# Reordering the opening of a convolution and maxout feed-forward kernel: products, zeroing, casts and two loads

## The chip, the core and the metric

The kernel runs on one core of a Trainium2 chip. TensorE multiplies matrices into PSUM; VectorE, ScalarE and GpSimd do elementwise work on SBUF (VectorE and ScalarE also on PSUM); SyncE issues the transfers between HBM and SBUF. The engines run side by side, each through its own queue in order, and wait for each other on semaphores. The metric is the device time of one execution in microseconds. Before the change the median of three runs is 453.2 us (452.73 to 454.73).

## What is computed

A short causal convolution along the sequence, with a softmax over its seven taps for each of eight heads, feeds a three-way maxout layer and an output projection. Cut to what matters:

```python
# x: (8, 4160, 192), weight: (8, 7), w1, w2, w3: (192, 768), w_out: (768, 192)
w = softmax(weight, axis=-1)
x_pad = concat([zeros(8, 6, 192), x], axis=1)
y[b, s, h*24 + g] = sum(w[h, k] * x_pad[b, s + k, h*24 + g] for k in range(7))
y = y.reshape(33280, 192)
h = maximum(maximum(y @ w1, y @ w2), y @ w3)
out = h @ w_out          # (33280, 192), float32
```

## The kernel before, in words

The 33,280 tokens are cut into 65 blocks of 512. For every block the kernel makes y (the convolution), then six hidden tiles of 128 columns, then four output tiles of 128 tokens.

**The algebra.** max(y w1, y w2, y w3) is y w3 + max(relu(y(w1 - w3)), y(w2 - w3)). So `wd` holds w1 - w3 and w2 - w3 as fp16 (made by `make_wd`, from the float32 weights in `wall`, whose parts are `ws` and `w3s`), and the y w3 w_out part is one 192x192 matrix `m16` made once: w3 is cast (`cast_w3`), transposed on TensorE (`transpose_w3`), multiplied by w_out (`make_m`) and copied out by ScalarE. A hidden tile takes two PSUM banks: ScalarE computes r = relu of one, VectorE takes the maximum with the other into h (`top`). Stage 2 multiplies h by w_out and adds y m16.

**The 192 columns.** The 192 input channels are 128 plus 64. A full product uses 128 rows of the array; the remaining 64 channels of both factors run as two half-height products side by side. `wd` therefore has slots 0 and 1 (first 128 channels of either factor), slot 2 (the last 64 of both, one in each half of the partitions) and slot 3, in which `cross_wd` puts copies of parts of slots 0 and 1 in the other half. For slot 2 w3 must stand in both partition halves: `copy_w3` does that. Blocks 0 and 1 use the full-height "first products" (`l1_dense` part "F") and half-height "third products" (part "H"); from block 2 on, `l1` uses half-height products throughout, and so needs slot 3 and the same kind of copy of y (`cross`).

**The opening.** Blocks 0 to 3 are loaded dense (`load_x`), cast to fp16 with zeros between channels (`cast_dense`, into two buffers `xz`, shared by blocks 0 and 2, and by 1 and 3), convolved by matmuls with a band matrix in two halves (`conv_dense`, tile D; the first half holds channels 0 to 127) and evacuated to `yd`. Blocks 4 onward are loaded into seven rotating buffers `xf`, some rows of which must be zeroed before the load (`zero_x`), then cast by GpSimd (`cast_x`), convolved (`conv`), evacuated and turned by a transposing transfer (`turn`). `first_hidden` is stage 2 of block 0 (24 products of h and w_out), `first_rest` adds the y m16 part later. `keep_warm` issues idle matmuls at the very start.

**What sets the order.** The order is written out by hand for the opening: each engine executes its instructions in program order. In the loop that follows, two lanes of half-height products are interleaved by column count. All loads are on SyncE's queue, in order; an issue waits until the transfer eight issues earlier is complete, and a load of x4 to x7 also waits for its buffer's zeroing. PSUM is three pools: psp and psq with two banks each, psw with four. `PQ` names psp and psq; `WW` names psw twice.

Before the change, the opening runs in this order: first differences of weights, conv 0, zeroing of x6, loads of x4 to x6, cast of block 1 by GpSimd and ScalarE, first products of block 0's hidden tiles 0 and 1, conv 1 (second half first), third products of those tiles, block 1's tiles 0 and 1, then tiles 2 and 3 and tiles 4 and 5 of both blocks, the transposition of w3, stage 2 of block 0, conv 2, m, and the loop.

Of the kernel before, what the change touches and what calls it, by code (L numbers as in the profile page):

```python
# [28 lines left out]
def kernel(  # L29
# [12 lines left out]
    nc = tc.nc  # L42
# [3 lines left out]
    H, KWs = weight.shape  # L46
# [39 lines left out]
    NDENSE = 4  # L86
# [3 lines left out]
    NR = NBLK // TOK // 2  # L90
# [28 lines left out]
    xin, xbuf, XBUF, loaded = {}, [], 7, set()  # L119

    def get_x(t):

        if not 0 <= t < NB or t in xin:
            return
        if t < XBUF:
            xbuf.append(const.tile([P, NR, D], FP32, name=f"xf_{t}"))
        xf = xbuf[t % XBUF if t < NDENSE + XBUF else NDENSE + (t - NDENSE - XBUF) % 3]
        assert all(v[0] is not xf for v in xin.values())
        xin[t] = [xf, 0, ()]

    def zero_x(t, q0=0, q1=NR, eng=None):

        if t >= NDENSE:
            get_x(t)
        xf = xbuf[t]
        if eng is not None:
            eng.memset(xf[TOK:HALF, q0:q1, :], 0.0)
            return
        zero = idle[TOK:HALF, 0:D]
        nc.scalar.copy(out=xf[TOK:HALF, q0:q1, :],  # L140
                       in_=bass.AP(tensor=zero.tensor, offset=zero.offset,
                                   ap=[list(zero.ap[0]), [0, q1 - q0], [1, D]]))

    def load_x(t, eng=nc.sync):
        if not 0 <= t < NB:
            return
        loaded.add(t)
        get_x(t)
        xf = xin[t][0]
        if t < NDENSE:  # L150
            todo = [(0, c[3], c[1] * SEQ + c[2], i) for i, c in enumerate(chunks_of[t])]
        else:
            todo = [(HALF * (i // NR) + (0 if s else LAP), KR if s else TOK,
                     b * SEQ + s - (LAP if s else 0), i % NR) for i, (b, s) in enumerate(rows_of(t))]
        parts = []
        i, n = 0, len(todo)
        row = [c[2] for c in todo]
        while i < n:
            k = i
            while k + 1 < n and todo[k + 1][:2] == todo[i][:2] and row[k + 1] - row[k] == row[i + 1] - row[i]:  # L160
                k += 1
            step = row[i + 1] - row[i] if k > i else 0
            p0, rlen, _, q0 = todo[i]
            q1 = todo[k][3] + 1
            src = bass.AP(tensor=x.tensor, offset=row[i] * D,
                          ap=[[D, rlen], [step * D, q1 - q0], [1, D]])
            eng.dma_start(out=xf[p0:p0 + rlen, q0:q1, :], in_=src)  # L167
            if parts and parts[-1][0] == rlen:
                parts[-1] = (rlen, parts[-1][1], q1)
            else:  # L170
                parts.append((rlen, q0, q1))
            i = k + 1
        xin[t] = [xf, todo[0][0], parts]
# [33 lines left out]
    def cast_dense(t, copies, slots_=range(CYC // 32)):  # L207
        xf, _, parts = xin.pop(t)
        for v, copy in enumerate(copies):
            if copy is None:  # L210
                continue
            for s in slots_:
                cut = GRP * (32 * s // GRP + 1)
                a, b = (32 * s, cut) if v == 0 else (cut, 32 * s + 32)
                for (rl, q0, q1) in parts:
                    copy(  # L216
                        out=xz[t][v][0:rl, q0:q1, :].rearrange("p q (k c) -> p q k c", c=CYC)[:, :, :, a:b],
                        in_=xf[0:rl, q0:q1, :].rearrange("p q (k c) -> p q k c", c=CYC)[:, :, :, a:b])
# [8 lines left out]
    def load_wa(f):  # L227
        for st, n, wsrc in ((w3s, 0, moe_w3), (ws, 0, moe_w1), (ws, 1, moe_w2)):
            nc.sync.dma_start(out=st[:, n, f], in_=wsrc[0:P, f])  # L229
# [15 lines left out]
    load_wa(slice(PW, 2 * PW))  # L245
    load_wb(slice(PW, DFF))
    load_wa(slice(2 * PW, DFF))
    nc.sync.dma_start(out=wos[:], in_=moe_w_out.rearrange("(j p) c -> p j c", p=P))
    load_x(2)
    load_x(3)  # L250
    ident = const.tile([P, P], FP32)
    make_identity(nc, ident[:])
# [36 lines left out]
    for lo, hi, copy in ((0, CUT, nc.scalar.copy), (CUT, WIN, nc.vector.tensor_copy)):  # L289
# [6 lines left out]
        for a in range(4):  # L296
            copy(out=band[32 * a:32 * a + 32, :, 32 * a + lo:32 * a + hi],
                 in_=bps[:, 0:hi - lo, :].rearrange("p c h -> p h c"))
    zero_x(5)
    keep_warm((NBLK,) * 3, psp, "p")  # L300


# [7 lines left out]
    def make_wd(n, j0, j1, eng=nc.vector):  # L310
        f = slice(P * j0, P * j1)
        eng.tensor_sub(out=wd[:, n, f], in0=ws[:, n, f], in1=w3s[:, n // 2, f])

    def copy_w3(copy, j0, j1):
        f = slice(P * j0, P * j1)
        copy(out=w3s[HALF:P, 1, f], in_=w3s[0:HALF, 1, f])
# [5 lines left out]
    def cross_wd(i, copy):  # L322
        copy(out=wd[HALF * i:HALF * (i + 1), NC, :], in_=wd[HALF * (1 - i):HALF * (2 - i), i, :])
# [52 lines left out]
    def conv_dense(t, copies, pools=((None, None),) * 2, order=(0, 1)):  # L376


        yd = dense[t] = ydp.tile([P, NC, NBLK], FP16, tag="yd", name=f"yd_{t}")
        for n in order:  # L380
            slots_ = ((0, 1, 2, 3), (4, 5, 4, 5))[n]
            pool, tag = pools[n]
            ps = (pool or psw).tile([P, NBLK], FP32, tag=tag or "w", name=f"D{n}_{t}")
            for (q, b, row_lo, rlen, lo, hi, cc) in chunks_of[t]:
                for v in range(2):
                    for g, s in enumerate(slots_):
                        h = (32 * s + 31 * v) // GRP
                        nc.tensor.matmul(  # L388
                            ps[32 * g:32 * g + 32, lo:hi],
                            lhsT=xz[t][v][0:rlen, q, 32 * s:32 * s + 32],  # L390
                            rhs=band[0:rlen, h, cc:cc + hi - lo],
                            start=(v == 0), stop=(v == 1), tile_position=(0, 32 * g))
            copies[n](out=yd[:, 2 * n, :], in_=ps[:])

    def cross(t, *copies):

        yd = dense[t]
        for i, copy in enumerate(copies):
            copy(out=yd[HALF * i:HALF * (i + 1), 1, :], in_=yd[HALF * (1 - i):HALF * (2 - i), 0, :])
# [127 lines left out]
    def l1_dense(tiles, parts="FH"):  # L527

        meet()
        for part in parts:  # L530
            order = [(i, v) for i in range(2) for v in tiles] if part == "F" else [(i, v) for v in tiles for i in range(2)]
            for i, (t, j, pools) in order:
                pool, tag = pools[i]
                if (t, j, i) not in open_ps:
                    open_ps[t, j, i] = pool.tile([P, NBLK], FP32, tag=tag, name=f"l{tag}{i}_{t}_{j}")
                    begun.discard((t, j, i))
                if part == "F":
                    a, b = wd[:, i, P * j:P * (j + 1)], dense[t][:, 0, :]
                else:
                    a, b = w_of(i, NC - 1, j), y_all(t, i, NC - 1)  # L540
                nc.tensor.matmul(open_ps[t, j, i][:], lhsT=a, rhs=b,  # L541
                                 start=(t, j, i) not in begun, stop=(t, j, i) in begun)
                begun.add((t, j, i))

    def tops(*tiles):
        for t, j in tiles:
            top(t, j, (open_ps[t, j, 0], open_ps[t, j, 1]), t == 1 and j % 2 == 1)
# [139 lines left out]
    PQ = ((psp, "p"), (psq, "q"))  # L687
    WW = ((psw, "w"), (psw, "w"))
    WPWQ = ((psw, "w"), (psp, "p"), (psw, "w"), (psq, "q"))
    ACT, DVE = nc.scalar.copy, nc.vector.tensor_copy  # L690
    GP = nc.gpsimd.tensor_copy
    make_wd(0, 0, 2)
    make_wd(1, 0, 2)
    zero_x(6, 4, NR, nc.vector)
    conv_dense(0, (ACT, DVE))
    zero_x(6, 0, 4)
    for t in range(NDENSE, XBUF):
        load_x(t)
    copy_w3(DVE, 0, 2)
    make_wd(2, 0, 2)  # L700
    cast_dense(1, (GP, ACT), (1, 2, 0))
    l1_dense([(0, 0, PQ), (0, 1, PQ)], "F")
    cast_w3(0, 2)
    copy_w3(GP, 2, 6)
    make_wd(2, 2, 4, nc.gpsimd)
    for n in range(NC):
        make_wd(n, 4, 6, nc.gpsimd)
    cast_w3(2, 6)
    conv_dense(1, (DVE, ACT), order=(1, 0))
    make_wd(0, 2, 4)  # L710
    make_wd(1, 2, 4)
    cross_wd(0, GP)
    GP(out=wo[:], in_=wos[:])
    l1_dense([(0, 0, PQ), (0, 1, PQ)], "H")
    tops((0, 0), (0, 1))
    l1_dense([(1, 0, WW), (1, 1, WW)], "HF")
    tops((1, 0), (1, 1))
    l1_dense([(0, 2, PQ), (0, 3, PQ)], "FH")
    tops((0, 2), (0, 3))
    l1_dense([(1, 2, WW), (1, 3, WW)], "HF")  # L720
    tops((1, 2), (1, 3))
    l1_dense([(0, 4, PQ), (0, 5, PQ)], "FH")
    tops((0, 4), (0, 5))
    cast_dense(2, (GP, GP))
    l1_dense([(1, 4, WW), (1, 5, WW)], "HF")
    tops((1, 4), (1, 5))
    transpose_w3((PQ[0], PQ[0], PQ[1]))
    cast_dense(3, (GP, GP))
    cross_wd(1, ACT)
    first_hidden(0)  # L730
    first_hidden(1)
    conv_dense(2, (ACT, DVE), (WW[0], PQ[1]))
    cast_x(4)
    cross(2, ACT, DVE)
    make_m(0)
    make_m(1)
    zero_x(0, NQ)
# [112 lines left out]
```

## Time and profile before

| Quantity | Value |
|---|---|
| Median of three runs | 453.2 us (452.73 to 454.73) |
| Profiled execution, its own time | 452.5 us |
| Its span | 450.7 us |
| TensorE busy | 444.7 us |
| VectorE busy | 356.5 us |
| ScalarE busy | 320.3 us |
| GpSimd busy | 204.0 us |
| Transfers | 72.01 MB, mean 160 GB/s |

The profile page lists busy time by engine, then the span in forty slices (a digit is the busy share of a slice in tenths), then the chain of work that ended last, by engine and line. PE is a matmul on TensorE, PEld its weight load, DVE is VectorE, ACT ScalarE, POOL GpSimd and SPq SyncE's queue. In the timelines a row has a start, a duration in us, the engine, line, operation, the tile written, the tile read and the shapes; in brackets stands how long the engine was idle just before and what ended that. The chain in order of time has a start, a duration and the work. Matmul ends are modelled, so a TensorE shown as busy can still be waiting a little.

### The profile page before, as it was taken

To read this page: it belongs to the slowest core of one execution; us is meant where nothing else is said; L and a number is where in the kernel's file an instruction comes from. 1 tells how busy PE (TensorE), PEld (TensorE's weight loads), DVE (VectorE), ACT (ScalarE), POOL (GpSimd) and SP (SyncE) were. 2 spreads that over 40 slices of the span, in tenths; PEclk is the share of its full clock that TensorE was granted. 3 is DMA by queue.
4 is the path that set the end of the run, shared out by engine and by line. 5 is a ranking of instruction groups with operands and counts; after the bars stand their busy time and mean duration, and the time that the engine had idled before them with its cause. 6 is when DMAs were issued, how large, how long until landed. Compare 5 with 4: busy or idle time off the path is not lost.

```text
span 450.7 us, 18261 instructions
## 1 busy us (share of the span) xinstructions
PE 444.7 (99%) x7576; PEld 409.5 (91%) x7576; DVE 356.5 (79%) x610; ACT 320.3 (71%) x600; POOL 204.0 (45%) x234
## 2 busy tenths in 40 slices
PE   7999999999999999999999999999999999999997
PEld 4579999999999999999999999999999999999996
DVE  7778778878778787787887887887887887887775
ACT  7977677767677676776776777776776776776664
POOL 2874836556464524714724635526544545124000
PEclk9999999999999999999999999999999999999999
DMA  7978999495977759649559749769549566172123
GB/s 204 238 191 158 208 183 240 134 217 148 183 208 161 184 107 214 172 112 205 158 138 185 190 103 193 192 105 218 157 116 207 160 157 151 48 139 75 56 71 106
DMA packets 128242, 72.01 MB, mean 160 GB/s; under 512 B 52320, under 2 KB 127967, under 8 KB 128159
## 3 DMA queue, kind: packets, MB, share of 16 engines
q1 hardware_dynamic: 127999, 70.75, 68.8%
q8 instruction: 59, 0.97, 1.0%
q14 instruction: 24, 0.20, 0.2%
q10 hardware_dynamic: 160, 0.10, 0.1%
HBM read 33.28 MB, written 25.56 MB: 131 GB/s over the span
## 4 chain that ended last, share of the span: by engine, by line
PE 97%; DMA 1%; SPq 1%; issue 0%; DVE 0%; POOL 0%; POOLq 0%
PE po L582 36%; PE lq L517 32%; PE lp L517 22%; PE G L367 3%; PE lw L541 1%; DMA xf<-in_x_dram 1%; PE D L388 1%; PE lp L541 1%; PE po L613 0%; PE po L640 0%; SPq L233 0%; SPq L229 0%; PE pm L347 0%; PE lq L541 0%; SPq L167 0%; PE pt L338 0%
## 5 line engine op out<-in xcount | busy, mean ns | idle before, releaser
L582 PE MATMUL po<-wo,h 64*128 64x192 f16 x3024 | 331.7, 243 | 0.0
L505 DVE TENSOR_TENSOR h<-r,lq 128x512 f16<-128x512 f16 x384 | 263.0, 686 | 84.3 <-ACT r L500 74.3
L500 ACT ACTIVATE r<-lp 128x512 f16<-128x512 f32 x384 | 229.0, 597 | 113.4 <-PE lp L517 103.0
L517 PE MATMUL lp<-yp,wd 64*128 64x512 f16 x1098 | 295.6, 376 | 0.0
L517 PE MATMUL lq<-yp,wd 64*128 64x512 f16 x1098 | 295.5, 376 | 0.0
L582 PEld LDWEIGHTS <-h 64*128 64x128 f16 x3024 | 242.6, 94 | 5.5 <-issue 4.1
L517 PEld LDWEIGHTS <-wd 64*128 64x128 f16 x2268 | 181.6, 94 | 14.9 <-issue 0.2
L199 POOL CAST x<-xf 103x768 f16<-103x768 f32 x122 | 97.2, 825 | 112.4 <-DMA xf<-in_x_dram 108.9
L582 PE MATMUL po<-m,yp 64*128 64x192 f16 x720 | 140.3, 243 | 0.0
L430 POOL COPY yp<-yp 64x1536 f16<-64x1536 f16 (+1 forms) x70 | 90.9, 1298 | 87.3 <-DMA yp<-ys 62.3
L590 DVE TENSOR_TENSOR o<-a,po 128x384 f32<-128x384 f32 x126 | 69.0, 548 | 0.0
L582 PEld LDWEIGHTS <-yp 64*128 64x128 f16 x720 | 66.3, 94 | 0.1
L589 ACT COPY a<-po 128x384 f32<-128x384 f32 x126 | 59.5, 472 | 0.0
L407 ACT CAST ys<-G 128x480 f16<-128x480 f32 (+1 forms) x53 | 25.4, 530 | 9.5 <-PE G L367 9.5
L407 DVE CAST ys<-G 128x480 f16<-128x480 f32 (+1 forms) x53 | 30.2, 610 | 0.0
L367 PE MATMUL G<-x,band 39*32 39x240 f16 (+3 forms) x1024 | 16.5, 242 | 0.0
L367 PEld LDWEIGHTS <-band 39*32 39x32 f16 x1024 | 10.2, 91 | 4.6 <-issue 4.1
L517 PE MATMUL lq<-yd,wd 64*128 64x512 f16 x36 | 9.7, 376 | 0.0
L517 PE MATMUL lp<-yd,wd 64*128 64x512 f16 x36 | 9.7, 376 | 0.0
L541 PEld LDWEIGHTS <-wd 128*128 128x128 f16 (+1 forms) x48 | 3.1, 96 | 6.0 <-issue 2.8
L216 POOL CAST xz<-xf 112x160 f16<-112x160 f32 (+2 forms) x15 | 4.3, 330 | 7.9 <-DMA xf<-in_x_dram 7.8
L388 PEld LDWEIGHTS <-xz 112*32 112x32 f16 x320 | 3.9, 96 | 2.7 <-POOL xz L216 1.1
(79 smaller groups left out, 98.1 us busy)
## 6 DMA issues: line engine op xcount, KB each, us to landing
xf<-in_x_dram SPq DMA_DIRECT2D x113, 234.0 KB
out_dram<-o SPq DMA_DIRECT2D x62, 384.0 KB
wall<-in_moe_w_dram SPq DMA_DIRECT2D x12, 128.0 KB
xf<-in_x_dram SPq DMA_DIRECT2D x7, 204.8 KB
xf<-in_x_dram SPq DMA_DIRECT2D x3, 420.0 KB
yp<-ys SPq DMA_TRANSPOSE x70
out_dram<-o SPq DMA_DIRECT2D x5, 192.0 KB
wos<-in_moe_w_out_dram SPq DMA_DIRECT2D x1, 576.0 KB
```

What stands on the lines that cost most here:

```text
L199: nc.gpsimd.tensor_copy(out=x16s[t0][0:K, :, :, u, r, :].rearrange("p h j c -> p j h c"), in_=xf[0:K, 4 * r:4 * r + 4, :].rearrange("p j ( ...
L367: nc.tensor.matmul(G[2 * (k // per) + i][TOK * j:TOK * (j + 1), k % per, :], lhsT=band[row, h, HALF * i + LAP:HALF * i + KR], rhs=x16s[t0] ...
L388: nc.tensor.matmul(ps[32 * g:32 * g + 32, lo:hi], lhsT=xz[t][v][0:rlen, q, 32 * s:32 * s + 32], rhs=band[0:rlen, h, cc:cc + hi - lo], star ...
L407: copy(out=slots[t][:, i % 2, :, :, GRP * h0:GRP * (h0 + per)].rearrange("p u r (h c) -> p h (u r) c", c=GRP), in_=G[i][:].rearrange("p h ...
L430: nc.gpsimd.tensor_copy(out=yp[HALF * i:HALF * (i + 1), 1, :, :, :, :].rearrange("p i u k n -> p (i u k n)"), in_=yp[HALF * (1 - i):HALF * ...
L500: nc.scalar.activation(out=r[:], in_=ps[0][:], func=AF.Relu)
L505: nc.vector.tensor_max(out=hs[t][:, j, :], in0=r[:], in1=q[:])
L517: nc.tensor.matmul(ps[i][:], lhsT=w_of(i, c, j), rhs=y_all(t, i, c), start=(n == 0), stop=(n == NC - 1))
L541: nc.tensor.matmul(open_ps[t, j, i][:], lhsT=a, rhs=b, start=(t, j, i) not in begun, stop=(t, j, i) in begun)
L582: nc.tensor.matmul(ps[b0, i][:, s % 2, :], lhsT=a, rhs=b, start=first, stop=last)
L589: nc.scalar.copy(out=a[:], in_=ps[s - 1, 0][:])
L590: nc.vector.tensor_add(out=outs[t][:, s - 1:s + 1, :], in0=a[:], in1=ps[s - 1, 1][:])
```

## The change

All of it lies in the first part of the kernel. On SyncE's queue the load of x2 goes ahead of the load of w_out. ScalarE zeroes x5 after block 0's first evacuation instead of before it; GpSimd zeroes all of x6, where VectorE and ScalarE each zeroed half. GpSimd, not VectorE, makes the first copy of w3. Block 1 is cast by GpSimd and VectorE instead of GpSimd and ScalarE. The third products of block 0's tiles 0 and 1 and their tops go ahead of conv 1, which now takes its first half first and is evacuated by ScalarE alone. Block 1's tiles 0 and 1 take first products before third. The second copy of w3 is split between GpSimd and ScalarE. On GpSimd the cast of block 2 goes ahead of the cast of w_out, and `cross_wd(0)` leaves GpSimd for ScalarE. Conv 2 and block 2's `cross` go ahead of `first_hidden`, with both `cross_wd` copies behind `cross` on ScalarE.

```diff
     load_wa(slice(2 * PW, DFF))
+    load_x(2)
     nc.sync.dma_start(out=wos[:], in_=moe_w_out.rearrange("(j p) c -> p j c", p=P))
-    load_x(2)
     load_x(3)
...
-    zero_x(5)
+    get_x(5)
     keep_warm((NBLK,) * 3, psp, "p")
...
     make_wd(1, 0, 2)
-    zero_x(6, 4, NR, nc.vector)
+    copy_w3(GP, 0, 2)
+    zero_x(6, eng=nc.gpsimd)
     conv_dense(0, (ACT, DVE))
-    zero_x(6, 0, 4)
-    for t in range(NDENSE, XBUF):
-        load_x(t)
-    copy_w3(DVE, 0, 2)
+    zero_x(5)
     make_wd(2, 0, 2)
-    cast_dense(1, (GP, ACT), (1, 2, 0))
-    l1_dense([(0, 0, PQ), (0, 1, PQ)], "F")
+    cast_dense(1, (GP, DVE), (1, 2, 0))
+    l1_dense([(0, 0, PQ), (0, 1, PQ)], "FH")
+    tops((0, 0), (0, 1))
+    conv_dense(1, (ACT, ACT))
+    make_wd(0, 2, 4)
+    make_wd(1, 2, 4)
     cast_w3(0, 2)
-    copy_w3(GP, 2, 6)
+    copy_w3(GP, 2, 4)
     make_wd(2, 2, 4, nc.gpsimd)
+    l1_dense([(1, 0, WW), (1, 1, WW)], "FH")
+    tops((1, 0), (1, 1))
+    copy_w3(ACT, 4, 6)
     for n in range(NC):
         make_wd(n, 4, 6, nc.gpsimd)
     cast_w3(2, 6)
-    conv_dense(1, (DVE, ACT), order=(1, 0))
-    make_wd(0, 2, 4)
-    make_wd(1, 2, 4)
-    cross_wd(0, GP)
+    cast_dense(2, (GP, GP))
     GP(out=wo[:], in_=wos[:])
-    l1_dense([(0, 0, PQ), (0, 1, PQ)], "H")
-    tops((0, 0), (0, 1))
-    l1_dense([(1, 0, WW), (1, 1, WW)], "HF")
-    tops((1, 0), (1, 1))
+    for t in range(NDENSE, XBUF):
+        load_x(t)
     l1_dense([(0, 2, PQ), (0, 3, PQ)], "FH")
...
     tops((0, 4), (0, 5))
-    cast_dense(2, (GP, GP))
...
     cast_dense(3, (GP, GP))
+    conv_dense(2, (ACT, DVE), (WW[0], PQ[1]))
+    cross(2, ACT, DVE)
+    cross_wd(0, ACT)
     cross_wd(1, ACT)
     first_hidden(0)
     first_hidden(1)
-    conv_dense(2, (ACT, DVE), (WW[0], PQ[1]))
     cast_x(4)
-    cross(2, ACT, DVE)
     make_m(0)
     make_m(1)
```

## The prediction

> **What bounds the kernel now.** I read the page's busy shares first, then the chain of waits, then the opening engine by engine.
>
> ```profile
> PE 444.7 (99%) x7576; PEld 409.5 (91%) x7576; DVE 356.5 (79%) x610; ACT 320.3 (71%) x600; POOL 204.0 (45%) x234
> ...
> PE   7999999999999999999999999999999999999997
> ...
> PE 97%; DMA 1%; SPq 1%; issue 0%; DVE 0%; POOL 0%; POOLq 0%
> ```
>
> TensorE is busy 99% and carries 97% of the chain; only the first and last slices of forty fall short. The change moves work in the first 25 us and removes no matmul, so its worth is the shift in time at which TensorE enters its unbroken run. The chain in order of time shows where that run begins:
>
> ```profile
> 5.05 4.31 DMA xf<-in_x_dram
> 9.49 0.34 POOL xz L216
> 9.87 1.30 PE D L388 x71
> 11.17 0.32 PE lp L541
> ...
> 22.72 1.10 PE pm L347 x12
> 23.81 0.37 PE lp L517
> ```
>
> From 9.87 the chain names only TensorE, but matmul ends are modelled, so I checked who stands close behind it. The timelines of the weight loads, GpSimd and ScalarE:
>
> ```profile
> 14.15 0.55 PEld L541 LDWEIGHTS <-wd 64*128 64x128 f16 x8 [0.47 <-POOL wd L312]
> ...
> 13.38 0.72 POOL L312 TENSOR_TENSOR wd<-wall 128x256 f16<-128x256 f32 x1 [0.20 <-DMA wall<-in_moe_w_dram]
> ...
> 17.38 1.08 ACT L500 ACTIVATE r<-lp 128x512 f16<-128x512 f32 x2 [0.26 <-PE lq L541]
> ...
> 21.42 0.83 ACT L323 COPY wd<-wd 64x768 f16<-64x768 f16 x1
> 22.32 0.59 ACT L393 CAST yd<-D 128x512 f16<-128x512 f32 x1
> 22.93 0.62 ACT L399 COPY yd<-yd 64x512 f16<-64x512 f16 x1
> 23.46 0.71 ACT L349 CAST m<-pm 128x192 f16<-128x192 f32 x2
> 24.20 0.67 ACT L140 CAST xf<-idle 32x576 f32<-32x576 f16 x1
> ```
>
> Two gates matter. Gate one: the third products of block 0's hidden tiles 2 and 3 (14.15) wait for a GpSimd subtraction, which waited for weights until 13.38. Gate two: block 2's first products (23.81) reuse the PSUM buffer that the first copy of m empties. That copy starts at 23.46 and the second shows at 23.85, so it ends as those products start; ScalarE shows no idle from 17.38 to there. TensorE's own work (pm, to 23.82) ends in the same instant.
>
> **Part one, up to gate one.** x5's zeroing (1.47 us on ScalarE, 6.11 to 7.58) no longer precedes block 0's copy, which started at 7.60; its half of conv 0 is done about 6.9. First products start near 7.5 instead of 8.24, and the third products (0.44: 11.10 to 11.54 before) run about 8.6 to 9.05, once VectorE's wd (0.42) follows its copy. But block 1's input lands at 9.4 whatever we do (GpSimd starts on it at 9.49), and gate one is set by weights queued ahead of everything that is swapped. So this head start is worth nothing unless TensorE would have been late at 14.15.
>
> It now nearly is. Before, conv 1 took its second half first and started 0.38 after the casts began; now its first half needs all three GpSimd casts (0.86, to 10.35) and VectorE's three. VectorE replaces ScalarE as the second caster, and it collides with GpSimd:
>
> ```profile
> 23.11 1.66 POOL L199 CAST x<-xf 103x768 f16<-103x768 f32 x2
> ...
> 23.49 0.58 DVE L399 COPY yd<-yd 64x512 f16<-64x512 f16 x1
> ...
> L505 DVE TENSOR_TENSOR h<-r,q x3: 444/514/767, 14.3 to 20.0; 128x512 f16<-128x512 f16 x3
> ```
>
> The VectorE copy that began at 23.49 ends at 24.07, 0.19 after the first of the two GpSimd casts gives way (23.88), and the same 128x512 maximum takes 0.44 or 0.77. VectorE's three cast shapes took 0.21, 0.27 and 0.18 on block 0 with GpSimd idle. So conv 1 starts between 10.35 (no collision) and 10.95 (all 0.6 serialized); I take 10.75, nearer the row of 23.49.
>
> [...]
>
> From 10.75: half of conv 1, 0.52 (1.03 whole, in the chain), a ScalarE copy 0.59 with both hand-offs, to 11.9; first products of block 1 with the switch 0.95 (16.00 to 16.95), third 0.45; first products of tiles 2 and 3 with their switches 1.05. TensorE reaches gate one at 14.35 instead of 14.15: **+0.2 us**, from 0 (cast end 10.35) to +0.4 (10.95).
>
> What may delay those casts further: GpSimd now copies w3 (half of a 0.61 row, 0.3) and zeroes all of x6 before them. No row shows 32x1536 zeroed by GpSimd. Its 128x1 and 128x128 memsets (0.11, 0.20) give 0.76 ns an element, 1.27 us; its 512-element copy (0.61) gives at most 1.83. The first weights land between 7.4 (bytes by stage: 1.02 MB wanted, moved by 6.4, plus the 1 us by which block 1's input trails the same count) and 8.89, where VectorE read them without waiting. At 7.4 the zeroing ends by 9.0 to 9.5: nothing. At 8.89 it ends at 10.5 to 11.0, conv 1 starts 1.0 to 1.5 later, and the products with it. I take the early landing, the one that two estimates of bytes support.
>
> **Part two, up to gate two.** cross_wd(0), 0.83 as ScalarE's own copy at 21.42 (0.91 on GpSimd before), joins ScalarE's queue between block 2's cross copy and m. ScalarE had no slack there: m, x0's zeroing and the first relu of block 2 all follow. It costs at least 0.67 (less 0.09 overlap, as 22.93 to 23.46 is 0.53 for a 0.62 copy, and less the 0.07 pause before 22.32) and at most 0.90 (start to start, 21.42 to 22.32). Mean of these, rounded down toward the overlapped row: **+0.75**. TensorE's conv 2 and stage 2 only trade places; both ended before pm, whose end does not move ahead of m. Behind m wait first_rest and all that follows.
>
> **Moves that I cost at nothing, with their cover.** x2 ahead of w_out: GpSimd finishes w3h at 17.32 and could not use x2 before; x2 takes the slot of a transfer that had landed by 18.35. Six casts (1.71, half of 3.42) end at 19.1, or 20.1 at worst, against conv 2's turn at 19.6; the loss would be swallowed by TensorE's later 0.75 wait. w_out then lands by 19.55, x2's old latest, is cast in 1.14 and is wanted at 20.7. Part of w3 copied by ScalarE (0.3) sits behind block 1's q; the 0.26 pause at 17.38 covers it, and the GpSimd subtraction that waits for it starts at 15.6. Block 1's second evacuation on ScalarE ends near 12.5, wanted at 12.85. VectorE sheds 0.70 of zeroing, takes 0.6 of casts, and delivers wd near 12.95 for 13.4. On SP, x7's load waits for x0's zeroing about 1 us longer; behind it stand block 0's store, x8 and the first transposes (30.85), while x7's cast has until conv 7 at 42.5. x4 to x6 are issued by 20.6, waiting on zeroings done by 11.
>
> **Sum.** 0.2 + 0.75 = 0.95. The profiled execution took 452.5 (span 450.7 and 1.8 around it), so 453.45; it stood 0.7 below the median 453.2, on which the forecast is **454.15 us**, own range 453.9 (0.67 alone) to 454.5 (0.4 + 0.90).
>
> **Rivals.**
> *No new wait.* Casts don't collide and m's copy still comes in time: for it speaks that pm's end and the products' start coincide, so the trace cannot say that ScalarE alone gates; against it, ScalarE's unbreaking queue. Then 453.2; with weights landing half a microsecond earlier 452.9; with half of cross_wd exposed 453.6. This is also the case that the change does nothing it seems to: the earlier first products buy no time because x1 and weights, both untouched, end the wait.
> *GpSimd's zeroing sits in front of x1.* Decided by the first weights landing after about 7.9. At 8.89: 1.0 to 1.5 more, 455.1 to 455.7.
> *TensorE goes cold, the slower side.* Between third products (9.05) and conv 1 (10.75) it idles 1.7 us; the longest gap now is 0.9. Seven warm-up matmuls of 2,880 columns took 2.58 us, 0.90 ns a column, against 0.42 later (0.22 for 512), though the profile's clock row shows 1.00. If the gap brings that pace back for a stretch as long as at the start (1.2 to 4.9), half of 3.7 is lost: 1.85, 456.0. It decides if 512-column matmuls after 10.75 start 0.43 apart. Against it: gaps of 0.9 and 0.6 us left the pace whole.
>
> [...]
>
> **How the numbers follow.** Chances: forecast 0.58; no new wait 0.17; zeroing in front 0.12; cold 0.08; an unseen gain over 0.5% 0.05. Half a per cent is 2.27 us, about what a measurement of this kernel tells from no change; the bounds are 450.9 and 455.5. Slower takes cold and half of the zeroing case, 0.14; faster 0.05; the same 0.81. The range, 452.7 to 455.7, holds the forecast, the second case and most of the third and leaves out cold and the unseen gain, under 0.2.
>
> **What would show it.** First products near 7.5; third products before conv 1; conv 1 starting 10.35 to 10.95, with VectorE and GpSimd casts lengthened; tiles 2 and 3's third products at 14.15 to 14.6; two 0.83 copies in a row on ScalarE; m 0.67 to 0.90 later relative to w3t; block 2's first products near 24.8. A GpSimd memset ending after 9.5, matmuls at 0.43, or products at 23.8 or earlier would prove me wrong.

## The result, and the profile after

The changed kernel takes 455.37 us in the median of 22 executions (454.06 to 457.56), the kernel before 453.44 beside it (452.45 to 454.73). The ratio is 1.0042, 95% interval 1.0032 to 1.0053: 1.9 us slower. The ratio lies inside the half per cent that counts as no change, its interval reaches a little beyond. The forecast was 454.15 with a range of 452.7 to 455.7; the time lies in the range, 1.2 above the forecast.

The times are of two kinds. Every execution is listed with the TensorE clock that was granted on average over it. In 11 of the 22 it is 0.999 or 1.000, and they take 454.68 on average (standard error 0.17); in the other 11 it is 0.995 or 0.996, and they take 456.12 (0.23). The mean of before in that comparison is 453.46 (0.14). So every execution lost about 1.2 us, and half of them 1.4 more: 1.23 + 0.5 x 1.44 = 1.95. Of before, the later comparisons list 105 executions with their clock, none under 0.999. The two parts differ in kind, and they are taken one after the other.

The profiled execution is one at full clock: 454.85 us, span 453.1. First the page of the changed kernel: busy shares, TensorE's forty slices, and the chain that ended last by engine.

```profile
PE 444.9 (98%) x7576; PEld 409.6 (90%) x7576; DVE 356.2 (79%) x610; ACT 320.3 (71%) x599; POOL 204.8 (45%) x235
...
PE   6999999999999999999999999999999999999997
...
PE 95%; ACT 1%; DMA 1%; SPq 1%; issue 1%; DVE 0%; DVEq 0%; ACTq 0%
```

TensorE is as busy as before in microseconds (444.9 against 444.7). What grew is the part of the chain that it does not carry, and only the first slice, some 11 us, shows less of it. The chain of the changed kernel in order of time (start, length, what):

```profile
10.71 0.62 DVE xz L216
11.33 0.04 issue
11.37 0.65 PE D L388 x30
...
12.68 1.56 PE lw L541 x8
...
17.31 0.69 DVE h L505
18.00 0.04 issue
18.04 0.38 PE lq L541
...
21.32 1.47 ACT w3t L341 x3
22.79 0.50 ACT yd L393
...
23.31 0.62 ACT yd L399
23.92 0.73 ACT wd L323
24.66 0.03 issue
24.68 0.52 ACT wd L323
25.20 0.34 issue
25.53 0.33 ACT m L349
25.86 0.04 issue
25.90 0.37 PE lp L517
```

Before, nothing but TensorE stood in it from 9.87 to 23.81. Now other engines do. VectorE's cast of block 1's input stands ahead of conv 1, and VectorE's maximum at 17.31 ahead of a product of tiles 4 and 5. From 18.78 on the chain stays in ScalarE's queue: relus, the copies of w3t (the transposed w3, taken out of PSUM), the evacuation of conv 2, the two cross_wd copies, and m. The timelines of the engines (start, busy, engine, line, operation; in brackets the idle time before it and what ended it) show what stands behind each:

```profile
6.75 1.37 POOL L137 MEMSET xf<- 32x1536 f32 x1
9.71 1.61 DVE L216 CAST xz<-xf 112x160 f16<-112x160 f32 x3 [1.22 <-DMA xf<-in_x_dram]
9.76 0.89 POOL L216 CAST xz<-xf 112x160 f16<-112x160 f32 x3 [1.64 <-DMA xf<-in_x_dram]
10.60 0.66 POOL L320 CAST w3h<-wall 128x512 f16<-128x512 f32 x1
...
15.64 0.40 ACT L316 COPY wall<-wall 64x256 f32<-64x256 f32 x1
16.07 1.09 ACT L500 ACTIVATE r<-lp 128x512 f16<-128x512 f32 x2
16.12 0.72 POOL L312 TENSOR_TENSOR wd<-wall 128x256 f16<-128x256 f32 x1 [0.99 <-ACT wall L316]
18.04 0.38 PE L541 MATMUL lq<-yd,wd 128*128 128x512 f16 x1 [0.22 <-DVE h L505]
...
23.83 1.68 ACT L323 COPY wd<-wd 64x768 f16<-64x768 f16 x2
25.53 0.54 ACT L349 CAST m<-pm 128x192 f16<-128x192 f32 x2
25.90 0.37 PE L517 MATMUL lp<-yd,wd 64*128 64x512 f16 x1 [0.77 <-ACT m L349]
```

GpSimd's zeroing of x6 takes 1.37 and ends at 8.12, well ahead of block 1's input at 9.7. VectorE's three casts take 1.61 where the same three took 0.66 on block 0 before. They run into GpSimd's three and then into its cast of w3h. ScalarE's copy of w3 pushes the relus of tiles 2 and 3 to 16.07, and GpSimd's subtraction waits 0.99 for it. The two cross_wd copies put m 4.35 behind the first copy of w3t (21.18 to 25.53), against 3.66 before (19.80 to 23.46), and TensorE waits 0.77.

Marks of before and after in the profiled executions: third products of tiles 2 and 3 (gate one) 14.16 and 15.14; the transposition pt that follows them 18.80 and 20.19; first products of block 2 (gate two) 23.81 and 25.90. So +0.98 at gate one (0.27 of it because block 1's input landed at 9.71 instead of 9.44), +0.41 from there to pt, +0.70 from pt to gate two. Together 2.09, more than the 1.2 by which full-clock executions differ on average; the profiled execution of before was a favourable one: 452.5, 0.96 under the mean.

### The profile page after: what moved, and what is told of

Read it like the earlier page. It is cut to its first block, busy times and chain, and to the rows that moved or that the text cites. A ratio compares the mean times of both kernels' runs of the same rounds, so it can differ in the third digit from the quotient of the medians.

```text
span 453.1 us, 18263 instructions
## 1 busy us (share of the span) xinstructions
PE 444.9 (98%) x7576; PEld 409.6 (90%) x7576; DVE 356.2 (79%) x610; ACT 320.3 (71%) x599; POOL 204.8 (45%) x235
## 4 chain that ended last, share of the span: by engine, by line
PE 95%; ACT 1%; DMA 1%; SPq 1%; issue 1%; DVE 0%; DVEq 0%; ACTq 0%
PE po L582 36%; PE lq L517 31%; PE lp L517 22%; PE G L367 3%; DMA xf<-in_x_dram 1%; PE lw L541 1%; PE po L640 0%; SPq L233 0%; PE D L388 0%; ACT w3t L341 0%; PE lp L541 0%; SPq L229 0%; ACT wd L323 0%; ACT r L500 0%; ACT yd L393 0%
## 5 line engine op out<-in xcount | busy, mean ns | idle before, releaser
L388 PE MATMUL D<-band,xz 112*32 112x103 f16 (+1 forms) x320 | 4.6, 209 | 2.6 <-POOL xz L216 1.6
```

Of the source, the lines that this page charges most:

```text
L388: nc.tensor.matmul(ps[32 * g:32 * g + 32, lo:hi], lhsT=xz[t][v][0:rlen, q, 32 * s:32 * s + 32], rhs=band[0:rlen, h, cc:cc + hi - lo], star ...
```

## The experiments

The account to be tested (theory A in the texts on record) is that these three waits make the time: the cast collision, ScalarE's copy of w3, and cross_wd(0) on ScalarE. The rivals put it elsewhere: in the swap of x2 and w_out, in conv 2's new place, in GpSimd's zeroing, or in a slow TensorE. Each experiment changes one thing, or a few of these parts together, in the kernel after or in the kernel before; two repeat these kernels as they are. A table with all of them stands at the end of this section.

**e1: block 1's second caster is ScalarE again.**

```diff
-    cast_dense(1, (GP, DVE), (1, 2, 0))
+    cast_dense(1, (GP, ACT), (1, 2, 0))
```

> The changed kernel with one part undone: block 1 is cast by GpSimd and ScalarE again, not GpSimd and VectorE. Theory A (VectorE's and GpSimd's casts get in each other's way, so conv 1 runs at 11.37 instead of about 10.7): conv 1 runs unbroken from about 10.7; ScalarE's relus of block 0 move behind its casts, so its first evacuation is at about 11.6 instead of 12.04; the third products of tiles 2 and 3 start at about 14.7 instead of 15.14, and block 2's first products at about 25.45 instead of 25.90; the time falls by 0.4 to 0.7 us. Theory B (block 1's input simply lands later after the swap of loads, 9.71 against 9.44, and all else follows): conv 1 still waits past 11, block 2's first products stay within 0.1 of 25.90.

Measured: 453.89 us, 1.0012 (1.0002 to 1.0021). Conv 1 runs in one piece; the timeline of e1:

```profile
10.36 1.10 PE L388 MATMUL D<-band,xz 112*32 112x103 f16 x80 [1.21 <-POOL xz L216]
```

Gate one is back at 14.17 and block 2's first products come at 24.94 instead of 25.90, though about 0.3 of that is an earlier landing. The median fell by more than the marks do, 1.5 us, and the clock says why: all 12 executions are at 1.000. Against the full-clock executions of the kernel after, e1 (453.91 on average) gains 0.55 to 0.77 (454.46 in e8's comparison, 454.68 in the first). The rest is the half clock, which is gone as well.

**e9: the same casts by ScalarE and VectorE, GpSimd left out.** It takes away the collision and keeps VectorE as caster.

```diff
-    cast_dense(1, (GP, DVE), (1, 2, 0))
+    cast_dense(1, (ACT, DVE), (1, 2, 0))
```

> The changed kernel with block 1 cast by ScalarE and VectorE, none of it by GpSimd: it asks whether VectorE is slow at these casts or only beside GpSimd. Theory A (they get in each other's way): VectorE's three casts take 0.6 to 0.7 us together as on block 0, or up to 1.25 if GpSimd's cast of w3 (0.6) runs at that moment, against 1.61; conv 1 runs from about 10.2 to 10.4 unbroken; the third products of tiles 2 and 3 start near 14.4; the time falls by 0.5 to 1.2 us from the changed kernel's. Theory B (VectorE alone is slow at these shapes): they still take over 1.3 us and conv 1 still breaks off.

Measured: 453.89 us, 1.0016 (1.0006 to 1.0026), all 11 executions at 0.999 or 1.000. The timeline of e9:

```profile
9.20 0.55 DVE L216 CAST xz<-xf 112x160 f16<-112x160 f32 x3 [0.71 <-DMA xf<-in_x_dram]
...
10.01 1.11 PE L388 MATMUL D<-band,xz 112*32 112x103 f16 x80 [0.87 <-ACT xz L216]
```

VectorE's three casts take 0.55 here and 1.61 beside GpSimd. That settles the collision: same engine, same instructions, only GpSimd's work is away. In after VectorE's single casts took 0.24, 0.92 and 0.60, the first two while GpSimd's casts ran, the last while its w3h cast did; the same three shapes had taken 0.21, 0.27 and 0.18 on block 0 in before.

**e5: the other way round, only the casters of block 1 changed in the kernel before.**

```diff
-    cast_dense(1, (GP, ACT), (1, 2, 0))
+    cast_dense(1, (GP, DVE), (1, 2, 0))
```

> The kernel before with one part of the change alone: block 1 is cast by GpSimd and VectorE instead of GpSimd and ScalarE. Theory A (the two casters get in each other's way, as in the changed kernel, where VectorE's three casts took 1.61 us instead of about 0.6): conv 1 finds its last cast near 11 instead of 10.35, the third products of tiles 2 and 3 start 0.5 to 0.9 later than 14.15, block 2's first products at 24.3 to 24.7 instead of 23.81, and the time rises by 0.5 to 0.9 us. Theory B (the late conv 1 of the changed kernel comes from its order, first half first, and from late landings): products within 0.2 of 23.81.

Measured: 454.10 us, 1.0009 (0.9996 to 1.0021). VectorE's casts take 1.60 again, conv 1 starts at 9.86 and comes to a stop twice (10.48, 11.09), gate one falls to 15.65 and block 2's first products to 25.27. By the trace the collision costs more here than after; by the times it is +0.44 (standard error 0.25) in the 10 executions at full clock. Two more are at 0.996. On the median alone this run is inconclusive.

**e2: cross_wd(0) on GpSimd again, behind the casts of w3.**

```diff
     cast_w3(2, 6)
+    cross_wd(0, GP)
     cast_dense(2, (GP, GP))
...
-    cross_wd(0, ACT)
     cross_wd(1, ACT)
```

> The changed kernel with cross_wd(0) done by GpSimd again, between its cast of w3 and its cast of block 2; ScalarE has one such copy left. Theory A (ScalarE's queue alone delays m, and with it block 2's first products): m starts 0.7 earlier against the first copy of w3t; block 2's first products start at about 25.15 instead of 25.90, where TensorE's pm ends; the time falls by 0.7 us. GpSimd casts block 2 about 0.9 later, to 20.5, still ahead of conv 2 at 20.95. Theory B (TensorE's own order, conv 2 before stage 2, makes pm late): products stay at 25.9.

Measured: 453.86 us, 1.0015 (1.0001 to 1.0029). From the first copy of w3t to m: 20.91 to 24.53, 3.62, where before had 3.66 and after 4.35. The products start at 24.90 as pm ends. Four of the 12 executions are at 0.996, as the collision is still there. The other eight (453.64) lie 0.8 to 1.0 below the full-clock executions of after.

**e10: in the kernel before, cross_wd(0) moved to ScalarE, directly ahead of cross_wd(1).**

```diff
-    cross_wd(0, GP)
     GP(out=wo[:], in_=wos[:])
...
+    cross_wd(0, ACT)
     cross_wd(1, ACT)
```

> The kernel before, with cross_wd(0) moved from GpSimd to ScalarE directly ahead of cross_wd(1), and nothing reordered behind it: the price of that copy by itself. Theory A (ScalarE has no slack between the relus and m): the stretch from the start of the first copy of w3t to the start of m is 0.65 to 0.85 longer than the 3.66 of the kernel before, unless conv 2 itself is late; block 2's first products start that much after pm's end; the time rises by 0.5 to 0.9 us. Theory B (the cost in the experiment that moved both copies behind the cross copy came from that place in the order alone): stretch within 0.2 of 3.66 and the time within 0.3 us.

This is the cleanest price of that copy in a trace: up to pt at 18.80 every mark is within 0.02 of before. The timeline of e10:

```profile
21.42 1.69 ACT L323 COPY wd<-wd 64x768 f16<-64x768 f16 x2
...
24.27 0.52 ACT L349 CAST m<-pm 128x192 f16<-128x192 f32 x2
```

The copies start at 21.42, exactly where the single one stood before; m comes at 24.27 instead of 23.46, block 2's first products at 24.63 instead of 23.81, and the last stage 2 (445.86 before) at 446.68: +0.82 at each. In time it is 453.45, 1.0007 (0.9996 to 1.0019), and the mean lies only 0.24 (standard error 0.17) above before, under the 0.5 to 0.9 expected. So 0.82 is the price in a favourable execution, and most executions pay less; e12 below shows a pause of ScalarE that can cover part of the copy.

**e6: both cross_wd behind cross(2) in the kernel before.** I meant it as the same price, but it moves more than I wanted.

```diff
-    cross_wd(0, GP)
...
-    cross_wd(1, ACT)
     first_hidden(0)
...
     cross(2, ACT, DVE)
+    cross_wd(0, ACT)
+    cross_wd(1, ACT)
```

> The kernel before with one part of the change alone: cross_wd(0) moves from GpSimd to ScalarE, and both cross_wd copies go behind block 2's cross copy. Theory A (ScalarE's queue gates m, so its 0.83 is paid in full less an overlap): m starts 0.65 to 0.85 later against the first copy of w3t, TensorE stops between pm and block 2's first products, which start at 24.4 to 24.7 instead of 23.81; the time rises by 0.6 to 0.9 us. Theory B (ScalarE had slack here that the trace does not show): within 0.2 of 23.81.

Measured: 454.65 us, 1.0028 (1.0018 to 1.0038), +1.3 and more than expected. ScalarE in e6:

```profile
22.91 0.59 ACT L393 CAST yd<-D 128x512 f16<-128x512 f32 x1 [1.77 <-PE D L388]
...
24.06 1.68 ACT L323 COPY wd<-wd 64x768 f16<-64x768 f16 x2
```

Before, cross_wd(1) filled the wait for conv 2. Here ScalarE stands idle 1.77 in it and does both copies afterwards (x2 came late as well in this execution: GpSimd waited 0.92 for it, until 20.58). So a part of what e6 adds is the place of cross_wd(1); e10 was made to take that out. In the changed kernel the copies have the same place on ScalarE, but conv 2 runs ahead of stage 2, and its evacuation follows w3t without a pause.

**e3: ScalarE's copy of w3 given back to GpSimd.**

```diff
-    copy_w3(GP, 2, 4)
+    copy_w3(GP, 2, 6)
...
-    copy_w3(ACT, 4, 6)
```

> The changed kernel with the whole second copy of w3 done by GpSimd again, and none by ScalarE. Theory A (ScalarE's 0.40 copy sits ahead of the relus of tiles 2 and 3, VectorE frees the next PSUM bank late, and TensorE stops at 18.04): the stretch from the third products of tiles 2 and 3 to the transposition of w3 is 4.65 instead of 5.05, block 2's first products start at about 25.5, the time falls by 0.4 us. Theory B (that stretch was lengthened by something else, or the copy is covered by ScalarE's pause): the stretch stays above 4.95.

Measured: 454.95 us, 1.0030 (1.0015 to 1.0044). The stretch from gate one to pt is 14.87 to 19.52, 4.65, as before (4.64), and 5.05 in each of after, e8, e2, e1 and e9, which keep the copy. So the copy stretches it by 0.41. In this execution the gain went elsewhere; its timeline:

```profile
21.34 1.15 POOL L714 CAST wo<-wos 128x1152 f16<-128x1152 f32 x1 [0.97 <-DMA wos<-in_moe_w_out_dram]
...
22.54 2.14 PE L613 MATMUL po<-wo,h 128*128 128x192 f16 x24 [1.08 <-POOL wo L714]
```

w_out landed only at 21.34, and TensorE waited 1.08 for its cast; the products came at 25.61. The median is held up by six of 12 executions at 0.996. The other six take 454.23, 0.23 to 0.45 less than those of after: the size of the copy, but hardly more than the errors.

**e4 and e11: three, then two of the parts undone.** e4 is the edits of e1, e2 and e3 together; e11 is those of e1 and e2.

> All three parts undone at once: block 1 cast by GpSimd and ScalarE, cross_wd(0) and the whole second copy of w3 by GpSimd. Theory A (three waits in a row that add): block 2's first products at about 24.3 (25.90 less 0.45, 0.4 and 0.7), so the time is within 0.5 us of the kernel before. Theory B (one of them shadows the others): no earlier than the best single one, about 25.1, and the time stays more than 1 us above the kernel before.

> The changed kernel with block 1 cast by GpSimd and ScalarE and cross_wd(0) on GpSimd, the second copy of w3 still split: the two larger terms undone. Theory A (they carry nearly all of the loss): the third products of tiles 2 and 3 near 14.2, no stop of TensorE ahead of block 2's first products, the time within 0.4 us of the kernel before; what ScalarE's copy of w3 still costs shows as a stretch of 4.9 to 5.1 from those third products to the transposition of w3, against 4.65. Theory B (the loss lies in the rest of the reordering): the time stays over 0.8 us above the kernel before.

Measured: e4 453.58 us, 1.0008 (0.9996 to 1.0020); e11 453.28, 1.0006 (0.9995 to 1.0017). None of these 24 executions is under 0.999. Block 2's first products come at 24.19 and 24.27, and e11 keeps the longer stretch to pt (14.25 to 19.29, 5.04), as it should. e4, without the copy, has 4.91 and not 4.65: TensorE's lq products at 16.52 took 0.85 there, against 0.59 at 16.43 in before, and the next ones came later; what held them up stays open. With two or three of the parts undone, what is left of the change cannot be told from nothing. That e4 is no faster than e11 means that the copy of w3 has no price that the times could show. The gains do not simply add: against the full-clock executions of after, e1 gains 0.55 to 0.77 and e2 0.8 to 1.0, and e11, which is both, 1.0 to 1.2. e4's profiled execution had a stop of TensorE of 1.25 us behind conv 3, put down to nothing that the profile shows, in none of the others; I leave it open.

**e7: x2 ahead of w_out, conv 2 and its cross ahead of stage 2, in the kernel before.**

```diff
-    nc.sync.dma_start(out=wos[:], in_=moe_w_out.rearrange("(j p) c -> p j c", p=P))
     load_x(2)
+    nc.sync.dma_start(out=wos[:], in_=moe_w_out.rearrange("(j p) c -> p j c", p=P))
...
     cross_wd(0, GP)
+    cast_dense(2, (GP, GP))
     GP(out=wo[:], in_=wos[:])
...
-    cast_dense(2, (GP, GP))
...
     cast_dense(3, (GP, GP))
+    conv_dense(2, (ACT, DVE), (WW[0], PQ[1]))
+    cross(2, ACT, DVE)
     cross_wd(1, ACT)
     first_hidden(0)
     first_hidden(1)
-    conv_dense(2, (ACT, DVE), (WW[0], PQ[1]))
     cast_x(4)
-    cross(2, ACT, DVE)
```

> The kernel before with the third group of moves alone: x2 loaded ahead of w_out and cast ahead of it, conv 2 and block 2's cross ahead of block 0's stage 2, cross_wd copies where they were. Theory A (these only trade places): block 2's first products within 0.2 of 23.81, the time within 0.3 us. Theory B (w_out, now the later transfer, comes too late for stage 2, as in the run in which its cast waited for it until 21.34 and TensorE stopped for 1.1 us): stage 2 starts up to 1.1 after conv 2 ends, products at up to 24.9.

Measured: 453.34 us, 0.9996 (0.9985 to 1.0008): no cost in the times. The marks of its trace cannot test it: the profiled execution was a late one (454.47; third weights at 16.35), and block 2's first products came at 25.81, beyond what either theory gave. It shows the collision at another place; the timeline of e7:

```profile
21.09 1.88 DVE L505 TENSOR_TENSOR h<-r,q 128x512 f16<-128x512 f16 x1
...
21.55 1.14 POOL L714 CAST wo<-wos 128x1152 f16<-128x1152 f32 x1
```

The maximum of 128x512 that takes 0.44 alone took 1.88, beside GpSimd's casts, and conv 2, fed by those casts, 2.00 instead of 1.10.

**e8: the changed kernel unaltered, once more.**

> The changed kernel once more, unaltered, for a second profiled execution: which of its late points are the kernel's and which one execution's. If the mechanism is the kernel's, VectorE's three casts of block 1 again take over 1.3 us, the third products of tiles 2 and 3 start at 14.85 to 15.2, and block 2's first products at 25.6 to 25.9; block 1's landing, 9.44 in the profile before and 9.71 in the first profile of the changed kernel, is expected to move between those by itself. If landings carried the loss, an execution with a landing at 9.44 would bring the third products back to about 14.3.

Measured: 454.85 us, 1.0035 (1.0020 to 1.0051); five of 12 executions at 0.995 or 0.996. The profiled one is of these: span 455.0, mean clock 0.996. It does the same work in the same order as after up to conv 1 (VectorE's casts 1.61 again), and then TensorE is slow. Stretches of e8; columns are stretch, its length, busy time and count of PE, PEld, DVE, ACT and POOL, then the granted clock, the share of the DMA engines and GB/s:

```profile
7.76:11.17 3.41, 1.59 (x12) 0.41 (x10) 2.27 (x6) 2.33 (x3) 1.87 (x5) 1.00 1.02 286
11.17:14.58 3.41, 3.32 (x80) 2.04 (x80) 1.90 (x5) 1.17 (x2) 1.83 (x3) 0.50 0.90 258
...
11.10:11.20 0.10, 0.00 (x0) 0.00 (x0) 0.10 (x2) 0.00 (x0) 0.05 (x1) 0.83 1.14 348
11.20:11.30 0.10, 0.04 (x4) 0.04 (x8) 0.10 (x2) 0.00 (x0) 0.00 (x0) 0.50 1.02 287
14.40:14.50 0.10, 0.10 (x2) 0.00 (x0) 0.00 (x0) 0.00 (x0) 0.10 (x1) 0.50 1.16 353
14.50:14.60 0.10, 0.10 (x1) 0.00 (x0) 0.00 (x0) 0.00 (x0) 0.10 (x1) 0.60 0.90 300
14.60:14.70 0.10, 0.10 (x1) 0.00 (x0) 0.00 (x0) 0.00 (x0) 0.10 (x1) 1.00 1.99 471
```

The clock falls to half at 11.17 (0.83 over the slice from 11.10: 0.066 of it whole) and comes back at 14.58: 3.41 us. Half of 3.41 lost, 1.7 of 455, is a mean clock of 0.996, the figure (or 0.995) by which these executions are known. The bulk of conv 1 (76 matmuls) and block 1's first products are slower for it, here in e8's timeline of TensorE:

```profile
11.26 1.83 PE L388 MATMUL D<-band,xz 112*32 112x103 f16 x76 [0.44 <-DVE xz L216]
13.02 2.33 PE L541 MATMUL lw<-yd,wd 128*128 128x512 f16 x8
```

In the execution at full clock these are 1.05 and 1.56. From the 76 matmuls to gate one it takes 4.99 instead of 3.77, so the half clock costs 1.22 there. Gate one comes at 16.25 instead of 15.14, and block 2's first products at 27.64 instead of 25.90; both are later than the text on record expected. The other 0.63 arises behind pt. A VectorE maximum took 2.14 beside GpSimd's casts, the next ones came late, and TensorE waited 0.86 for them; the timeline of e8:

```profile
19.75 2.14 DVE L505 TENSOR_TENSOR h<-r,q 128x512 f16<-128x512 f16 x1
...
20.47 1.15 POOL L715 CAST wo<-wos 128x1152 f16<-128x1152 f32 x1
...
22.54 0.61 PE L338 MATMUL pt<-ident,w3h 128*128 128x128 f16 x8 [0.86 <-DVE h L505]
```

**e12: the kernel before unaltered, once more.** It tells how far landings alone move the marks.

> The kernel before once more, unaltered, for a second profiled execution. It shows how far landings and the instruction supply move the marks from one execution to the next: block 1's casts start at 9.1 to 9.8, weights, w_out and x2 land up to 2 us later than in the first profile if the transfers vary as the profiles of the other kernels suggest; block 2's first products between 23.8 and 25; the time within 0.3 us of the kernel before. If the landings were the changed kernel's own doing, all of these marks would come out within 0.2 of the first profile.

Measured: 453.53 us, 1.0002 (0.9990 to 1.0014). Its profiled execution took 454.0 and has gate one at 14.75, pt at 19.39 (the stretch is 4.64 again) and block 2's first products at 24.80, 0.99 later than the first profile of before, with weights, w_out and x2 all waited for. ScalarE has a pause in it that the first profile did not have, behind cross_wd(1); its timeline:

```profile
22.01 0.83 ACT L323 COPY wd<-wd 64x768 f16<-64x768 f16 x1
23.30 0.58 ACT L393 CAST yd<-D 128x512 f16<-128x512 f32 x1 [0.46 <-PE D L388]
```

A second copy at that place would find 0.46 of its 0.83 covered, which goes with the 0.24 that e10 costs on average. A mark compared across two executions is thus good to about 1 us only; lengths between marks of one execution (the 4.64, 5.05, 3.66, 4.35) repeat far better.

The table sets the full-clock mean against the mean of before in the same comparison (standard errors of these differences 0.13 to 0.25), counts the executions at 0.995 or 0.996, and gives the least time that TensorE was busy in any 3.41 us (the length of e8's stretch at half clock) of the profiled execution that begin between 6.0 and 20.9, worked out from stretches of that length moved on by 0.1:

```
kernel                              full clock   at half    least busy
                                    less before  a while    in 3.41 us
after (first comparison)               +1.23      11 of 22     1.28
e8  after, again                       +1.05       5 of 12     1.51
e3  w3 copy on GpSimd                  +0.85       6 of 12     1.43
e2  cross_wd(0) on GpSimd              +0.27       4 of 12     1.77
e5  before, collision alone            +0.44       2 of 12     1.67
e1  no collision                       +0.53       0 of 12     1.96
e9  no collision, ACT and DVE          +0.51       0 of 11     2.19
e4  three undone                       +0.34       0 of 12     1.88
e11 two undone                         +0.04       0 of 12     2.29
e10 before, cross_wd(0) on ACT         +0.24       0 of 11     1.88
e6  before, both behind cross(2)       +1.35       0 of 11     2.16
e7  before, x2 and conv 2              +0.14       0 of 12     2.19
e12 before, again                      -0.12       0 of 12     1.74
before (in the later comparisons)         0       0 of 105    1.89
```

The half clock comes in the five rows in which VectorE casts block 1 beside GpSimd, and in no other.

## Why the prediction was right, and where it was wrong

That the change makes no difference of half a per cent was right on the median, and the time lies in the range. In part that is luck: the range was drawn to leave the half-clock case out, 8 of the 22 executions lie above its upper end of 455.7, and the median stays below it because only half of the executions had that case. The mechanism was right in both profiled executions of the changed kernel: the head start buys nothing, and block 2's first products wait for m, which waits for ScalarE. Point by point, by its steps:

- *The head start is worth nothing.* Right. First products at 7.59 (forecast near 7.5), third products from 8.55; conv 1 later all the same.
- *GpSimd's zeroing and copy end before x1 lands.* Right. The copy of w3 took 0.40 (forecast 0.3), the memset 1.37 (estimated 1.27, at most 1.83), done at 8.12.
- *Cast collision, +0.2, at most +0.4.* Right in kind, mis-sized. I put three GpSimd casts against three of VectorE and had conv 1 start at 10.75 and run through. VectorE lost time to a fourth GpSimd instruction, the cast of w3h behind them, and conv 1 went in two pieces: 4 matmuls at 10.71, 76 at 11.37. The path from there to gate one, 3.60 in the sum, took 3.77 to 3.92 (after, e1, e9). Measured: 0.98 at gate one, 0.7 without the later landing; in time 0.55 to 0.77 (e1 against after) and 0.44 (e5).
- *"the 0.26 pause at 17.38 covers it".* This step failed: ScalarE's copy of w3 is on the path. I looked for a pause behind it and not at the relus ahead of that pause. The copy delays them, VectorE's maximum waits for them, and TensorE's matmul at 18.04 waits for that. Measured by e3 and the repeated 5.05 against 4.65: +0.41 in the trace; in the times 0.2 to 0.45 at most, and by e4 against e11 nothing.
- *cross_wd(0) on ScalarE, +0.75, from 0.67 to 0.90.* Right in the traces: 0.69 in after, 0.82 alone in e10. In the times it is 0.8 to 1.0 in the changed kernel (e2 against after), but 0.24 (standard error 0.17) in the kernel before (e10). "ScalarE had no slack there" was read from one favourable execution; e12 has a pause of 0.46.
- *x2 ahead of w_out, conv 2 ahead of stage 2, nothing.* Right on the median (e7: 0.9996); the marks of e7's late execution do not show it. The cover is thin: a w_out that landed at 21.34 in e3 cost 1.08 there, where I had counted on 19.55.
- *"TensorE goes cold", chance 0.08, 456.0.* The weighing of this rival is the step that failed most: it came in 16 of 34 executions of the changed kernel. Its time came out by luck: those 16 have a median of 455.97, but from about 1.1 of waits and 1.5 of half clock, where I had 0.95 and 1.85 (the 16 take 456.14 on average, the other 18 454.60). I held it small because earlier gaps of 0.9 and 0.6 us had left the pace whole. The gap became 1.98 (1.55 and 0.43 around the four matmuls) instead of 1.7, as the casts collided for longer.

The only run at hand, that of before, had no gap between matmuls over 0.91, against the 1.7 foreseen, so the 0.08 was my estimate. What sets the half clock off is not shown by the later runs either. In e8 the clock fell to half at 11.17 and stayed there for 3.41 us; in the 3.41 us ahead of that TensorE was busy for 1.59. In the table the three rows that were hit most have 1.28 to 1.51 of busy time in a stretch of that length, the two that were hit less 1.67 and 1.77, the others 1.88 or more, but e12 with 1.74 and no hit does not fit in. Each of these figures is from one execution, and the one of after, with the least, 1.28, kept the full clock. So no bound is shown; what is shown is that the pair of casters brings the half clock and that removing either of the two (e1, e9) ends it: none of 23 executions had it.

So the 1.9 us are some 1.2 of waits (0.95 forecast) and 0.7 of a half clock in every other execution. No kernel that was run beat the one before; e4, e5, e7, e10 and e11 cannot be told from it.

## What to carry to other kernels

When a pair of VectorE and GpSimd instructions shares a moment, count every GpSimd instruction queued behind as a possible collider, not only those that start together: in after VectorE's last cast took 0.60 beside the w3h cast, where the same shape had taken 0.18 on block 0. A gap of TensorE early in a kernel is to be priced twice, the gap and the clock after it: here the gap was 1.98 us in after, and 16 of the changed kernel's 34 executions had a mean clock of 0.995 or 0.996. The longest pause does not foretell it: e5, with none above 0.9 us, had the half clock twice, and e1 and e4, with 1.21 and 1.28, never. TensorE's least busy time in 3.41 us goes better with it, 1.28 to 1.77 in the rows that were hit against 1.74 to 2.29 in the others, though no bound is shown. The mean granted clock of single executions tells it where one profile can miss it. Where a moved instruction is said to be covered by a pause, follow the instructions between its new place and that pause to whoever waits for them. And read the slack of an engine from more than one execution.

## What the runs showed that was not expected

- Beside GpSimd, VectorE can take three to five times as long: 0.55 to 1.61 for three casts, 0.44 to 1.88 (e7) and 2.14 (e8) for one maximum. GpSimd hardly slowed beside VectorE's casts in after (0.89 for its three, 0.85 in e1 beside ScalarE); its three took 1.04 to 1.11 in e5, e6, e7 and e10, where VectorE was subtracting weights meanwhile.
- One kernel has two times, 1.5 us apart, by whether the clock was halved for a while (3.41 us in e8, where it was profiled); the median lies between, so a profile of one execution shows only one of them.
- Landings differ between executions of one program: in before GpSimd took up w_out at 18.35 and block 2's input at 19.55 without a wait, in e12 it waited for them until 19.12 and 20.98. Across all kernels, the casts of block 1's input began between 9.07 and 9.71; GpSimd waited for the third weights until 16.35 in e7, and for w_out until 21.34 in e3.
